# Asking for the next weights nine products ahead instead of six, out of the same twelve buffers

## The chip, the cores and the metric

One core of a Trainium2 chip runs the whole program in one launch. The metric is device time in microseconds (us), smaller is better. Executions of the same program agree within a few tenths of a per cent.

## What is computed

Three stages in a row, all in float32 (the arrays of the last stage's weights come in as 64-bit floats and are turned into 32-bit ones on the core). Cut to what matters:

```python
# attention: 4 x 8 heads, 576 tokens, head size 64, chunks of 64 tokens
scores = scale * q_c @ k_c.T ; attn = softmax(scores) ; x = attn @ v_c      # -> x: 2304 x 512
# mixture of 4 experts, hidden width 1024 each
for e in range(4):
    h = maximum(x @ w1[e], 0)
    out += p[:, e:e+1] * (h @ w2[e])
# gated layer, width 1536
g = x @ w_gate
y = (silu(g) * (x @ w_val)) @ w_out
```

## The kernel before

**Passes, sets and products.** Tokens go through in passes of 768 (`TT` = 384, two halves). There are three passes of the expert stage and then three of the gated stage. A product `x @ W` on a block of 512 input and 256 output columns is done by a Strassen-Winograd scheme: seven products of half size instead of eight (`PRODUCTS`). One such block of weights in one pass is a *set*, and its seven products carry the places i = 0 to 6. Each operand is a sum of blocks of weights, kept as a high and a low part, so a product is six matmuls of 384 columns at L627, L628 and L629 (`half_k`), read from one *weight tile* of 256 KB. These tiles come from the pool `w` of twelve buffers (L789). `product` (L631) uses a tile and lets go of its buffer.

**Where the weight tiles come from.** In the first pass they are split on the core (`make_w`, L406) and stored to memory. In all later passes `load_w` (L413) loads them back with one DMA on the queue of SyncE, SP (issue at L415). The program is written out by hand: Python goes through the list `prods`, one *step* per product, and at each step it records the product, then work put off to this step by `later`, then `prepare` for the product `LEAD` = 6 steps on, and then some tasks. Each engine, and SP's queue of DMAs, does its own instructions strictly in the recorded order.

**A second user of the same twelve buffers.** During the second and third pass, tasks turn the 64-bit weights of the gated stage into split tiles (`make_ops`, L455). Each task loads a raw block on SP (L464) into a place that an earlier task must have left, converts it, and then makes seven tiles with `w_split` (L401), at most one tile a step. A made tile is also taken from the pool `w`. ScalarE (ACT) writes its high part at L125, GpSimd (POOL) its low part at L126, and three steps later SP stores it (L476):

```python
for a, to in stores:
    yield SPLIT
    t = w_split(r, a, f"made_{name}")
    later(3, lambda to=to, t=t: nc.sync.dma_start(to, t.bitcast(F32)))
```

There are 18 such groups of seven, 126 made tiles. A buffer can be written again once its product has run, or once its store has landed.

**What ACT owes TensorE (PE).** After products 0, 2 and 3 of a set ACT copies the sum out of PSUM (`keep`, L609, shown at L611: the tiles p, u and p again). Products 2, 4 and 5 then add into the same bank and have to wait for that copy. Between them stand other products and a gap of 18 matmuls of the second layer (y, L676 to L680; ox and oz at L743 in the gated stage).

**The change of pass.** Seven operands of the next pass's tokens are fetched raw (`x_fetch`, L205, issue at L208) into three buffers (pool `xt`, L1100) and split by ACT and VectorE (DVE) or POOL (`x_split`, L210). The first three are fetched ahead. Operand i + 3 is fetched two steps after product i of the last set, and operand i is split one step after that product, which frees a raw buffer.

**Other transfers on SP.** Second-layer weights of the experts (L515, L531) and of the gated stage (`fetch_wo`, L498, issue at L507), which wait for buffers that PE frees.

Of the kernel before, what the change touches and what calls it, by code (L numbers as in the profile page):

```python
# [91 lines left out]
def attention_moe_gated(  # L92
# [46 lines left out]
    def pass_of(n):  # L139
        part, s, _, _ = sets[n]  # L140
        return s + (NPASS if part == "two" else 0)

    def group_of(n):
        part, s, r, _ = sets[n]
        return (s * NPAIRS + r) // 2 if part == "one" else NPASS * NG1 + (s * NPAIRS2 + r) // 2
# [7 lines left out]
    def part_of(G):  # L153

        if G < NPASS * NG1:
            return (1, *divmod(G, NG1))
        return (2, *divmod(G - NPASS * NG1, NG2))

    now = [0]
    deferred = {}  # L160

    def later(d, f):
        deferred.setdefault(now[0] + d, []).append(f)
# [12 lines left out]
    def x_source(p, b):  # L176
        if b[0] == "b":
            return xs[p][int(b[2]) - 1, :, 2 * int(b[1]) - 2 : 2 * int(b[1])]
        return xt_d[p][int(b[1]) - 1]
# [25 lines left out]
    def x_fetch(p, i):  # L205
        b = PRODUCTS[i][2]
        t = x_raw[p, b] = xt_p.tile([P, 2, TT], F32, tag="xt", name=f"xraw_{b}_{p}")
        nc.sync.dma_start(t, x_source(p, b))  # L208
# [178 lines left out]
    def fetch_w1(n):  # L387
        r = raw1[n] = raw1_p.tile([P, 8, 2 * P], F32, tag="raw1", name=f"raw1_{n}")
        nc.sync.dma_start(r[:, 0:4], w1[weights_of(n)])

    def w_sums(r, engine=None, half=None):
        ops = (
            (S1, A21, A22, ALU.add),
            (S2, S1, A11, ALU.subtract),
            (S3, A11, A21, ALU.subtract),
            (S4, A12, S2, ALU.subtract),
        )
        for o, a, b, op in ops if half is None else ops[2 * half : 2 * half + 2]:
            (engine or nc.vector).tensor_tensor(out=r[:, o], in0=r[:, a], in1=r[:, b], op=op)  # L399
# [6 lines left out]
    def make_w(n, i):  # L406
        a = PRODUCTS[i][1]
        t = wop[n, i] = w_split(raw1[n], a, n)
        later(3, lambda: nc.sync.dma_start(w_d[weights_of(n)][i], t.bitcast(F32)))
        if i == NPROD - 1:  # L410
            del raw1[n]

    def load_w(n, i):  # L413
        t = wop[n, i] = w_p.tile([P, 2, 2 * P], F32R, tag="w", name=f"w_{n}_{i}")
        nc.sync.dma_start(t.bitcast(F32), w_d[weights_of(n)][i])  # L415
# [95 lines left out]
    def fetch_w2(G, j):  # L511
        part, s, g = part_of(G)
        if part == 1 and s > 0:
            t = w2op[G, j] = w2_tile(G, j)
            nc.sync.dma_start(t.bitcast(F32), w2_d[4 * g + j])  # L515
            return
        r = raw2[G, j] = raw2_p.tile([P, DM], F32, tag="raw2", name=f"raw2_{G}_{j}")
        nc.sync.dma_start(r, w2[4 * g + j])
# [148 lines left out]
    def layer2(G):  # L667

        for b in range(BLOCKS):
            pool, tag = y_places[b % len(y_places)]  # L670
            y = pool.tile([P, DM], F32, tag=tag, name=f"y_{G}_{b}")
            c = slice(b % HALF * P, (b % HALF + 1) * P)
            for j in range(4):
                hh, hl = hid[G, j, b // HALF]
                w = w2op[G, j]
                nc.tensor.matmul(y, hh[:, c], w[:, 0], start=(j == 0), stop=False)  # L676
                yield
                nc.tensor.matmul(y, hh[:, c], w[:, 1], start=False, stop=False)  # L678
                yield
                nc.tensor.matmul(y, hl[:, c], w[:, 0], start=False, stop=(j == 3))  # L680
                if j < 3:
                    yield
            gather(G, b, y)
            yield
# [99 lines left out]
    with tc.manual_schedule():  # L784
# [202 lines left out]
        def is_raw(n):  # L987
            return n < NPAIRS + 3
# [27 lines left out]
            later(1 + j, lambda j=j: first_split("t4", j))  # L1016
        later(2, lambda: split_w2(1, 1))

        FIRST, LEAD = 3, 6
        order = []  # L1020
        for n in range(FIRST, len(sets) + 1):
            for these in ((4, 5), (0, 1)), ((6,), (2, 3)):
# [4 lines left out]
        prods = [o for o in order if o is not None]  # L1027

        def last_of_pass(n):
            return 0 <= n < len(sets) - 1 and pass_of(n + 1) != pass_of(n)  # L1030

        def prepare(n, i):
            if is_raw(n):
                if i in (1, 3):
                    w_sums(raw1[n], half=i // 2)
                make_w(n, i)
                if i == NPROD - 1 and is_raw(n + 2):
                    fetch_w1(n + 2)
            else:
                load_w(n, i)  # L1040

        gap = 0
        for o in order:
            if o is None:

                gap += 1
                m = FIRST + (gap - 2) // 2
                G = group_of(m) - 1 if m >= FIRST else 0
                if G == 0:
                    for _ in range(12):  # L1050
                        next(two)
                elif part_of(G)[0] == 2:
                    if gap % 2 == 0 and group_of(m - 1) == G:
                        two = layer_out(G)
                    for _ in range(18):
                        next(two, None)
                else:
                    size = sum(group_of(k) == G + 1 for k in range(len(sets)))
                    if gap % 2 == 0 and group_of(m - 1) == G:
                        two = layer2(G)  # L1060
                    for _ in range(12 * BLOCKS // (2 * size)):
                        next(two)
                continue
            n, i = o
            p = pass_of(n)
            if o == (N1, 0):
                assert not tasks and not running, (len(tasks), len(running))
                raw64_cm.close()
                sg_p = ctx.enter_context(tc.tile_pool(name="sg", bufs=6, side="right"))
                wow_p = ctx.enter_context(tc.tile_pool(name="wow", bufs=2, side="right"))  # L1070
            product(n, i)
            if i == 0 and (n == FIRST or group_of(n) != group_of(n - 1)) and group_of(n) < NPASS * NG1:

                W = NPROD * sum(group_of(k) == group_of(n) for k in range(len(sets)))
                for j in range(2 if n == FIRST else 0, 4):
                    last = W + 2 if group_of(n) < NG1 - 1 else 5 + j * W // 4
                    begin, end = 1 + j * W // 4, 5 + j * W // 4 if j < 3 else last
                    if n == FIRST:
                        begin, end = 2 * j - 3, 4 * j - 3
                    later(begin, lambda G=group_of(n), j=j: fetch_w2(G, j))  # L1080
                    later(end, lambda G=group_of(n), j=j: split_w2(G, j))
            if last_of_pass(n + 1) and i == 5:
                for k in range(3):
                    x_fetch(p + 1, k)
            if last_of_pass(n):

                later(1, lambda p=p, i=i: x_split(p + 1, i))
                if i + 3 < NPROD:
                    later(2, lambda p=p, i=i: x_fetch(p + 1, i + 3))
            for f in deferred.pop(now[0], []):  # L1090
                f()
            if now[0] + LEAD < len(prods):
                prepare(*prods[now[0] + LEAD])
            if rest and now[0] % NPROD < 5:
                stage, a = rest.pop(0)
                stage(a, (psA, "a"))
                if not rest:
                    at_cm.close()
                    y_places.append((psA, "a"))
                    xt_p = ctx.enter_context(tc.tile_pool(name="xt", bufs=3, side="right"))  # L1100
                    w2x_p = ctx.enter_context(tc.tile_pool(name="w2x", bufs=1, side="right"))
                    raw64_cm = ExitStack()
                    raw64_p = raw64_cm.enter_context(tc.tile_pool(name="raw64", bufs=2, side="right"))
                    tasks.append(x_sums(1))
            if o == (NPAIRS + 2, 1):
                tasks += [x_sums(2)] + make64
            elif o == (2 * NPAIRS + 3, 1):
                tasks.insert(0, (y for p in (3, 4) for y in x_sums(p)))
            elif o == (N1 + 5, 4):
                tasks.append(x_sums(5))  # L1110
            elif o == (N1 + 3, 2):
                fetch_wo(NPASS * NG1, 0)
                fetch_wo(NPASS * NG1, 1)
            if not (last_of_pass(n) or last_of_pass(n + 1) and i >= 5 or now[0] - turned[0] < 2):
                run_tasks(2)
            now[0] += 1
# [69 lines left out]
```

## Time and profile before

| | |
|---|---|
| median of 3 runs | 1241.95 us (1239.88 to 1243.53) |
| the profiled execution's own time | 1239.78 us |
| its span in the trace | 1238.0 us |
| PE busy | 1223.6 us, 99% |
| DVE, ACT, POOL busy | 794.0, 538.4, 576.6 us |
| DMA queue of SP | 81.9% of 16 engines' span, 357 MB |
| TensorE clock granted | full speed in all 40 slices |

The span runs from the program's first instruction to its last. A matmul's recorded duration overlaps the next one's, so the engine's idle time and what ended it say more than its busy share. The second and third pass of the experts lie between about 355 and 840 us, the gated stage behind that.

### The profile page before, as it was taken

To read this page: it belongs to the slowest core of one execution; us is meant where nothing else is said; L and a number is where in the kernel's file an instruction comes from. 1 tells how busy PE (TensorE), PEld (TensorE's weight loads), DVE (VectorE), ACT (ScalarE), POOL (GpSimd) and SP (SyncE) were. 2 spreads that over 40 slices of the span, in tenths; PEclk is the share of its full clock that TensorE was granted. 3 is DMA by queue.
4 is the path that set the end of the run, shared out by engine and by line. 5 is a ranking of instruction groups with operands and counts; after the bars stand their busy time and mean duration, and the time that the engine had idled before them with its cause. 6 is when DMAs were issued, how large, how long until landed. Compare 5 with 4: busy or idle time off the path is not lost.

```text
span 1238.0 us, 21120 instructions
## 1 busy us (share of the span) xinstructions
PE 1223.6 (99%) x7216; PEld 1130.2 (91%) x7216; DVE 794.0 (64%) x1360; ACT 538.4 (43%) x1192; POOL 576.6 (47%) x603
## 2 busy tenths in 40 slices
PE   8999999999999999999999999999999999999998
PEld 6888888899888999898889889999999999999998
DVE  6776666666646766765566656455667756685576
ACT  4453434445424454544354344334435344444331
POOL 5554434477517776847376867301432222222221
PEclk9999999999999999999999999999999999999999
DMA  7587786799797999897899999866898797698874
GB/s 239 169 285 269 267 280 226 242 320 354 266 354 270 366 323 351 308 390 268 290 367 331 344 396 310 301 214 229 297 321 297 269 322 262 245 327 293 275 235 154
DMA packets 179562, 359.94 MB, mean 291 GB/s; under 512 B 19184, under 2 KB 46320, under 8 KB 179456
## 3 DMA queue, kind: packets, MB, share of 16 engines
q1 hardware_dynamic: 178528, 357.12, 81.9%
q10 hardware_dynamic: 896, 1.44, 0.4%
q8 instruction: 58, 0.95, 0.3%
q14 instruction: 48, 0.39, 0.1%
q0 software_dynamic: 32, 0.04, 0.0%
HBM read 258.90 MB, written 99.61 MB: 290 GB/s over the span
## 4 chain that ended last, share of the span: by engine, by line
PE 87%; DMA 4%; DVE 3%; issue 2%; ACT 2%; POOL 2%; SPq 1%; POOLq 0%; DVEq 0%; ACTq 0%
PE y L676 10%; PE y L680 10%; PE y L678 9%; PE lx L627 8%; PE lx L629 8%; PE lx L628 8%; PE ox L743 5%; PE oz L743 4%; PE lz L627 4%; PE lz L629 4%; PE lz L628 4%; PE lw L627 2%; PE lw L629 2%; PE lw L628 2%; DMA w<-w 1%
## 5 line engine op out<-in xcount | busy, mean ns | idle before, releaser
L676 PE MATMUL y<-w,hh 128*128 128x512 f32 x576 | 228.2, 396 | 0.0
L680 PE MATMUL y<-w,hl 128*128 128x512 f32 x576 | 226.5, 393 | 0.0
L678 PE MATMUL y<-w,hh 128*128 128x512 f32 x576 | 225.8, 392 | 0.2 <-POOL w L126 0.2
L126 POOL TENSOR_TENSOR ol<-sg,oh 128x384 fp32r<-128x384 f32 x72 | 80.0, 1121 | 307.1 <-ACT oh L125 260.0
L126 POOL TENSOR_TENSOR w<-raw,w 128x256 fp32r<-128x256 f32 (+1 forms) x156 | 143.5, 936 | 149.1 <-ACT w L125 131.7
L562 ACT ACTIVATE hh<-sum_p 128x384 fp32r<-128x384 f32 x90 | 47.2, 525 | 221.9 <-DVE sum_p L615 221.9
L766 DVE SCALAR_TENSOR_TENSOR acc<-y,prob,acc 128x512 f32<-128x512 f32 x126 | 91.2, 744 | 65.7 <-PE y L680 65.6
L680 PEld LDWEIGHTS y<-w,hl 128*128 128x128 f32 x576 | 108.1, 188 | 24.0
L676 PEld LDWEIGHTS y<-w,hh 128*128 128x128 f32 x576 | 108.3, 188 | 21.4 <-issue 1.4
L678 PEld LDWEIGHTS y<-w,hh 128*128 128x128 f32 x576 | 108.3, 188 | 21.2 <-POOL w L126 0.6
L615 DVE TENSOR_TENSOR sum_p<-lx,p 128x384 f32<-128x384 f32 x81 | 45.0, 555 | 93.0 <-PE lx L629 93.0
L563 DVE SCALAR_TENSOR_TENSOR hl<-sum_p,hh 128x384 fp32r<-128x384 f32 x90 | 61.7, 685 | 61.8 <-ACT hh L562 61.8
L126 POOL TENSOR_TENSOR w_made<-raw,w_made 128x256 fp32r<-128x256 f32 x84 | 68.1, 818 | 65.5 <-ACT w_made L125 53.0
L125 ACT ACTIVATE w<-raw 128x256 fp32r<-128x256 f32 (+1 forms) x156 | 67.6, 454 | 5.4 <-DVE raw L399 2.3
L125 ACT ACTIVATE oh<-sg 128x384 fp32r<-128x384 f32 x72 | 36.5, 525 | 70.4 <-DVE sg L576 70.1
L611 ACT COPY u<-lx 128x384 f32<-128x384 f32 x81 | 38.6, 476 | 64.5 <-PE lx L629 64.3
L627 PE MATMUL lz<-b22h,w 128*128 128x384 f32 x162 | 55.9, 345 | 0.9 <-ACT p L611 0.8
L627 PE MATMUL lz<-t1h,w 128*128 128x384 f32 x162 | 55.4, 342 | 1.2 <-DMA w<-w 1.1
L627 PE MATMUL lw<-b21h,w 128*128 128x384 f32 x162 | 54.8, 338 | 0.8 <-DMA w<-w 0.7
L627 PE MATMUL lx<-t2h,w 128*128 128x384 f32 x162 | 55.0, 340 | 0.0
L629 PE MATMUL lx<-t3h,w 128*128 128x384 f32 x162 | 54.9, 339 | 0.0
L615 DVE TENSOR_TENSOR sum_p<-lw,p 128x384 f32<-128x384 f32 x81 | 44.8, 553 | 15.8 <-PE lw L629 12.7
(273 smaller groups left out, 3384.6 us busy)
## 6 DMA issues: line engine op xcount, KB each, us to landing
w<-w SPq DMA_DIRECT2D x567, 256.0 KB, 5.4
w<-w SPq DMA_DIRECT2D x96, 512.0 KB, 6.1
w<-w_made SPq DMA_DIRECT2D x84, 256.0 KB, 5.8
wo_t<-wo_t SPq DMA_DIRECT2D x36, 512.0 KB, 5.1
wo_b<-wo_b SPq DMA_DIRECT2D x27, 512.0 KB, 4.1
raw<-w SPq DMA_DIRECT2D x19, 512.0 KB, 4.1
raw<-w SPq DMA_DIRECT2D x32, 256.0 KB, 4.4
sums<-x SPq DMA_DIRECT2D x40, 192.0 KB, 5.8
```

What stands on the lines that cost most here:

```text
L125: nc.scalar.activation(h, src, AF.Copy)
L126: (lo or nc.vector).tensor_tensor(out=l, in0=src, in1=h.bitcast(F32), op=ALU.subtract)
L563: nc.vector.scalar_tensor_tensor(out=l, in0=src, scalar=0.0, in1=h.bitcast(F32), op0=ALU.max, op1=ALU.subtract)
L615: nc.vector.tensor_tensor(out=t, in0=ps, in1=snap.pop(name), op=ALU.add)
L627: nc.tensor.matmul(ps, w[:, 0, c], xh[:, k], start=f, stop=False, skip_group_check=True)
L628: nc.tensor.matmul(ps, w[:, 0, c], xl[:, k], start=False, stop=False, skip_group_check=True)
L629: nc.tensor.matmul(ps, w[:, 1, c], xh[:, k], start=False, stop=e, skip_group_check=True)
L676: nc.tensor.matmul(y, hh[:, c], w[:, 0], start=(j == 0), stop=False)
L678: nc.tensor.matmul(y, hh[:, c], w[:, 1], start=False, stop=False)
L680: nc.tensor.matmul(y, hl[:, c], w[:, 0], start=False, stop=(j == 3))
L743: nc.tensor.matmul(o, left[:, c], w[:, k, right], start=start and t % 2 == 0 and k == 0 and i == 0, stop=k == 1 and i == 2, skip_group_che ...
L766: nc.vector.scalar_tensor_tensor(out=sum_, in0=y, scalar=p, in1=sum_, op0=ALU.mult, op1=ALU.add)
```

## The change

`prepare` for a product whose weights are loaded is called nine steps ahead. Where the weights are made (first pass), it stays at six. Since the list changes over from made to loaded, a counter `ready` says which product is next, and a step can prepare up to two. The pool `w` keeps its twelve buffers. At a change of pass, operand i + 3 is fetched four steps after product i instead of two; the split stays where it was.

```diff
-        FIRST, LEAD = 3, 6
+        FIRST, LEAD, LEAD_LOADS, X_WAIT = 3, 6, 9, 4
...
         gap = 0
+        ready = [LEAD]
...
                 if i + 3 < NPROD:
-                    later(2, lambda p=p, i=i: x_fetch(p + 1, i + 3))
+                    later(X_WAIT, lambda p=p, i=i: x_fetch(p + 1, i + 3))
             for f in deferred.pop(now[0], []):
                 f()
-            if now[0] + LEAD < len(prods):
-                prepare(*prods[now[0] + LEAD])
+            for _ in range(2):
+                if ready[0] < len(prods):
+                    if ready[0] <= now[0] + (LEAD if is_raw(prods[ready[0]][0]) else LEAD_LOADS):
+                        prepare(*prods[ready[0]])
+                        ready[0] += 1
```

The instructions on PE, DVE, ACT and POOL stand in the same order in both programs. Only SP's queue is in another order; on the other engines what changes is which buffer a weight tile gets, and so what its writer waits for.

**First place: SP's queue in the third make group of the gate weights, second pass.** `w_1` is the weight tile of a product with place 1, the number behind the arrow is the tile in memory, `w_made` a made tile, `raw_0` the raw block that starts a new task. Before:

```order
L515 DMA w_14_2_6017<-w_26_131 128x1024
L476 DMA w_97<-w_made_0_4_5960 128x512
L415 DMA w_0_6020<-w_91 128x512
L464 DMA raw_0_6027<-wg 128x1024 x2
L476 DMA w_97<-w_made_0_6_5981 128x512
L415 DMA w_1_6062<-w_91 128x512
L476 DMA w_97<-w_made_0_7_5999 128x512
L415 DMA w_6_6076<-w_90 128x512
```

With the change:

```order
L415 DMA w_1_5985<-w_91 128x512
L476 DMA w_97<-w_made_0_5_5924 128x512
L415 DMA w_6_6003<-w_90 128x512
L515 DMA w_14_2_6023<-w_26_131 128x1024
L476 DMA w_97<-w_made_0_4_5966 128x512
L415 DMA w_2_6026<-w_91 128x512
L464 DMA raw_0_6033<-wg 128x1024 x2
L476 DMA w_97<-w_made_0_6_5987 128x512
L415 DMA w_3_6068<-w_91 128x512
```

The load of `w_1` from tile 91 stood behind the raw block and a store; it now stands three loads earlier, ahead of both. Raw blocks and stores keep their places among themselves.

**Second place: SP's queue at the change from the first to the second pass of the gated stage.** `xraw` is a raw operand of the next pass: t1, t3, b22 and t4 in this order; `w_3_10949` is the weight tile of the product that uses t1. Before:

```order
L208 DMA xraw_t_4_10870<-xt_75 128x768
L415 DMA w_1_10880<-w_93 128x512
L208 DMA xraw_t_4_10890<-xt_75 128x768
L415 DMA w_6_10893<-w_104 128x512
L415 DMA w_2_10909<-w_93 128x512
L507 DMA wo_t_10911<-wo_t_2_152 128x1024
L208 DMA xraw_b_4_10943<-x_69 128x768
L415 DMA w_3_10949<-w_93 128x512
L208 DMA xraw_t_4_10960<-xt_75 128x768
```

With the change:

```order
L415 DMA w_3_10884<-w_93 128x512
L415 DMA w_4_10895<-w_93 128x512
L208 DMA xraw_t_4_10906<-xt_75 128x768
L415 DMA w_5_10913<-w_93 128x512
L507 DMA wo_t_10915<-wo_t_2_152 128x1024
L208 DMA xraw_t_4_10947<-xt_75 128x768
L415 DMA w_0_10953<-w_94 128x512
L415 DMA w_1_10972<-w_94 128x512
L208 DMA xraw_b_4_10983<-x_69 128x768
L415 DMA w_6_10991<-w_93 128x512
L208 DMA xraw_t_4_11003<-xt_75 128x768
```

The weights for t1 moved from behind the fetch of b22 to ahead of the fetch of t1. The fetch of t3 moved behind one transfer of second-layer weights (`wo_t`), and b22 behind two more loads of weights.

## Rows read from the trace of the kernel before

**Rows 1.** The page's head and part 1: busy us, share of the span, instructions.

```profile
span 1238.0 us, 21120 instructions
PE 1223.6 (99%) x7216; PEld 1130.2 (91%) x7216; DVE 794.0 (64%) x1360; ACT 538.4 (43%) x1192; POOL 576.6 (47%) x603
```

**Rows 2.** Waits of PE, 250 to 1200 us: us in total, times, longest us.

```profile
PE lz L627 <- DMA w<-w: 1.1, 1, 1.1
PE lz L627 <- ACT p L611: 0.8, 2, 0.5
PE lw L627 <- DMA w<-w: 0.7, 1, 0.7
```

**Rows 3.** Waits of PE's weight loads (PEld), whole span.

```profile
PEld lw L627 <- DMA w<-w: 1.4, 2, 1.0
```

**Rows 4.** Chain of waits, 500 to 530 us: start us, us, what.

```profile
516.78 0.71 POOL w_made L126
517.51 0.33 SPq L464
...
518.37 0.42 SPq L476
...
518.84 6.01 DMA w<-w
...
524.89 0.44 PE lw L627
```

**Rows 5.** Chain of waits, 700 to 718 us.

```profile
709.02 0.44 SPq L476
...
709.56 6.23 DMA w<-w
...
715.83 0.44 PE lw L627
```

**Rows 6.** Chain of waits, 944 to 962 us.

```profile
947.40 0.97 DVE t2l L126
...
948.39 6.41 DMA xraw_b<-x
...
954.82 0.85 ACT b22h L125
...
959.82 0.37 ACT p L611
...
960.24 0.44 PE lz L627
```

**Rows 7.** SP's queue in order of time, 940 to 962 us: start, us, instruction.

```profile
943.02 0.32 SPq L208 DMA_DIRECT2D xraw_t<-xt  x1
...
946.18 0.32 SPq L208 DMA_DIRECT2D xraw_t<-xt  x1
...
947.55 0.38 SPq L507 DMA_DIRECT2D wo_t<-wo_t  x1
948.39 0.32 SPq L208 DMA_DIRECT2D xraw_b<-x  x1
948.76 0.42 SPq L415 DMA_DIRECT2D w<-w  x1
```

**Rows 8.** Instructions of line L476: stores of made tiles, who waited, landing.

```profile
L476 SPq DMA_DIRECT2D w<-w_made x84: 319/320/1586, 394.4 to 793.8; - x84
...
  POOL w_made L126: 4.7, 2
  ACT w_made L125: 1.2, 2
...
DMA to landing us min/median/max: 2.0/5.8/8.2
```

**Rows 9.** Stretch 390 to 550 us: all engines, then L627 alone (two a product).

```profile
390.00:550.00 160.00, 159.88 (x800) 144.13 (x799) 110.28 (x166) 80.10 (x179) 118.45 (x124) 1.00 0.92 332
390.00:550.00 160.00, 48.58 (x145) 27.06 (x144) 1.00 0.92 332
```

**Rows 10.** PE and ACT in order of time, 508 to 516 us.

```profile
510.93 0.46 ACT L611 COPY p<-lx 128x384 f32<-128x384 f32 x1
511.28 0.42 ACT L125 ACTIVATE w_made<-raw 128x256 fp32r<-128x256 f32 x1
515.20 0.34 PE L627 MATMUL lx<-t2h,w 128*128 128x384 f32 x1
```

**Rows 11.** DMA issues by line: KB each, median us to landing.

```profile
xraw_t<-xt SPq DMA_DIRECT2D x20, 384.0 KB, 4.5
xraw_b<-x SPq DMA_DIRECT2D x15, 384.0 KB, 6.4
```

## Prediction

> **What bounds the kernel now.** I read the busy shares first. PE is busy for 1223.6 of 1238.0 us [rows 1], so only a change that reaches PE counts, and there is little to win. The next view is what PE waits for between 250 and 1200 us, the part in which weights are loaded and both changed numbers act. Its waits are short and few [rows 2]: 1.1 us once and 0.7 us once for a weight tile, 0.8 us in two pieces for ACT's copy p. The loads into the array show two waits for a weight tile at lw, 1.4 us together [rows 3]. I then followed the chain of waits back from each of these places. The two at lw have one cause. At 517.51 SP could issue a raw block (L464) only when POOL had finished a made tile at 517.49; the store and then the weight load stood behind it in the queue, so the load went out at 518.84, took 6.01 us, and PE started late at 524.89 [rows 4]. At 709.56 it was a store that held the queue, and PE started at 715.83 [rows 5]. The weights were late because SP's queue was blocked, not because memory was slow. The wait of 1.1 us lies at 954 us, in a change of pass: the weight load behind the fetch of b22 could go only at 948.76, since that fetch waited for the raw buffer that DVE freed with t2l at 948.37 [rows 6, 7].
>
> **Part 1: earlier loads.** The first place of the order shows that the load which was late at 524.89 now stands ahead of the raw block and both stores. The same holds for the one at 715.83, since every load moved three products forward. Three products are 6.6 us: in the stretch of 390 to 550 us L627 ran 145 times, two a product, so 72.5 products in 160 us, 2.2 us each [rows 9]. Both delays are smaller than that, so I take both away: **minus 1.4 us** [rows 3]. The bounds are nothing, if the freed buffers come too late to load earlier, and 1.4.
>
> The wait at 954 us goes too, because the weights for t1 now stand ahead of the fetch of t1. But what is late next is known. PE then runs up to b22, which needs ACT's copy p, and ACT makes that copy at 959.82, behind b22h, which waited for the raw operand until 954.80 [rows 6]. PE would be there 1.1 us sooner and wait 1.1 us longer. I count **0**; the upper end of the gain is the 1.1.
>
> **Part 2: raw operands two steps later.** In the second place of the order the fetch of t3 now stands behind `wo_t`, which went out at 947.55, where t3 had gone at 946.18 [rows 7]. That is some 1.8 us later with its own issue. b22 stands behind two more weight loads of 0.42 us each [rows 7], so about 0.9 us later, and the chain from b22 to PE at 960.24 has no slack [rows 6]. Against it stands its flight, 6.41 us in this chain, where operands t land in a median of 4.5 us and operands b in 6.4 [rows 6, 11]; fewer loads would be let go behind it at once. I take **0** here, nearest to the fact that the fetch still cannot start before DVE is done at 948.37. There are five changes of pass, so the bounds are minus 0.5 and plus 4.5 us (5 x 0.9).
>
> **Part 3: the made tiles lose their buffers.** This is the part of the change that the diff does not show. With a lead of six, six of twelve buffers hold weights that are waiting to be used, and six are left for made tiles. A made tile keeps its buffer for three steps until its store is issued, and until the store has landed, a median of 5.8 us [rows 8] or 2.6 products of 2.2 us [rows 9]. In a group of seven, one a step, that is 5.6 buffers: it fits. With a lead of nine, three are left, and 9 + 5.6 = 14.6 are wanted. So in 18 groups ACT and POOL, or SP's loads, must wait for a store to land. I counted the waits in the two built programs. Before, no split of a made tile waits for a store recorded in the same step or the step ahead of it; with the change 20 of 126 do, 12 of them in the same step.
>
> What does ACT's waiting cost PE? In one of these groups ACT copies p at 510.93 and starts a made tile at 511.28, and PE needs that bank at 515.20 [rows 10]. The copy was done at 511.39, so there are 3.8 us of cover at such a place. SP can issue the store at best when PE is through the product before, 2.2 us ahead of the split, since in the changed program most loads in front of the store wait for that product's buffer. The wait is then 5.8 - 2.2 = 3.6 us, just under the cover; with the longest landing, 8.2 us [rows 8], it is 6.0 us, 2.2 us over it. In the kernel before, waits for these stores came to 4.7 and 1.2 us and none reached PE [rows 8]. The bounds are therefore 0 and 12 x 2.2 = 26 us. I take two of the twelve at 1 us over the cover, **plus 2.0 us**, much nearer to the lower end, because a median landing stays covered. POOL's own waits I cost at nothing: it is busy for 118 of 160 us there [rows 9] and owes PE nothing in this stretch but the low parts of operands at a change of pass; without that cover its lag would show in the next group's start.
>
> The Trainium skill, in "DMA: Bandwidth & Descriptors", section "Anatomy of one DMA", puts a transfer at about 2.0 us plus its bytes over 436 GB/s, measured on another issuing path. An estimate from that page for 256 KB is 2.6 us, a buffer would then be held for 4.2 steps, every such wait would stay under the cover, and part 3 would cost nothing: the sum would be minus 1.4. The trace disagrees with the page for a queue this full: the median is 5.8 us and only the shortest, 2.0, comes near it [rows 8].
>
> **Sum.** Minus 1.4, plus 0, plus 0, plus 2.0: **plus 0.6 us** on the profiled execution's 1239.78 us, whose span of 1238.0 us leaves 1.8 outside. It is 2.2 us under the median of the runs, 1241.95. So I predict 1242.6 us.
>
> A measurement of this kernel can tell about 0.3%, 3.7 us; the lines are 1238.2 and 1245.7 us.
>
> **Rivals.**
> - *ACT and POOL are starved of buffers* (slower, 22%). The mechanism is part 3, in the groups between 390 and 800 us. It decides once the waits beyond the cover come to 5.1 us (3.7 + 1.4), 0.43 us for each of the twelve. At 0.6 us each it is 7 us, and the time is 1241.95 - 1.4 + 7 = 1247.6 us. For it: 14.6 buffers wanted of twelve, landings of up to 8.2 us. Against it: the cover, and that loads take part of the shortage, which nine ahead can bear.
> - *The raw operands come late* (slower, 6%). At each of five changes the 0.9 us reaches PE: with parts 1 and 3 as above, 1241.95 + 0.6 + 4.5 = 1247.0 us. Against it: the fetch waits for DVE anyway.
> - *All waits for memory go* (faster, 12%). PE's waits in the stretch are 1.4 + 1.1 + 0.8 = 3.3 us [rows 2, 3]. If all go and part 3 is free, the profiled execution comes to 1236.5 us and the median to 1238.6; it needs another 0.4 us from the median run, which has 2.2 us more to lose than the profiled one, to pass the line. About 1237.9 us then.
> - *The lead is not had* (no change, 12%). In the make groups the freed buffers come so late that the loads start no earlier than before: 12 - 5.6 = 6.4 buffers for loads is a lead of six again. Nothing of the 1.4 is won: 1241.95 + 2.0 = 1244.0 us.
>
> **How the numbers follow.** My forecast has 48%, and with the last rival "within 0.3%" has 60%; faster 12%; slower 28%. The range goes from 1238.8, nearly all waits gone, to 1248.0, just over the two slower cases. It leaves out about one in ten on each side.
>
> **What would show it.** Right: no wait of PE's lw for a weight tile between 250 and 840 us; waits of ACT and POOL at w_made for the stores (L476) grown from 5.9 us to tens of us; PE waiting for ACT's copies or for hl some 2 us more; the wait at 954 us moved to b22. Wrong on part 1: lw still waits. Wrong on part 3: PE's waits for ACT's copies p and u in 390 to 800 us come to over 5 us, or made tiles do not wait at all. Wrong on part 2: ACT's waits at b22h grow by more than 1 us at each change.

## The result, and the profile after

The change made the kernel slower: 1260.53 us (median of 4 runs, 1260.15 to 1261.82) against 1242.24 us for the kernel before on the same chip. The ratio is 1.0148, with a 95% interval of 1.0133 to 1.0163. The forecast was 1242.6 us, no change that could be told, and the range on record ended at 1248.0, so the prediction was wrong.

Where the time went is read from three views. The page's head and part 1 of the changed kernel answer to [rows 1]:

```profile
span 1260.0 us, 21223 instructions
PE 1231.7 (98%) x7216; PEld 1134.6 (90%) x7216; DVE 800.8 (64%) x1360; ACT 538.1 (43%) x1192; POOL 579.4 (46%) x603
```

The profiled span grew by 22.0 us (the medians differ by 18.3). An early group of matmuls of the gated stage dates it: the first ox<-wo_t began at 873.0 us before and at 895.3 us after, 22.3 us later. The next two rows show it, of the kernel before and of the changed one, from the instructions of line L743 (least, median and greatest duration in ns, then first and last start):

```profile
L743 PE MATMUL ox<-wo_t,oh x204: 276/279/385, 873.0 to 1225.5; 128*128 128x256 f32 x102
```

```profile
L743 PE MATMUL ox<-wo_t,oh x204: 276/279/387, 895.3 to 1247.4; 128*128 128x256 f32 x102
```

The stage's first sigmoid (sg, L570) was already as late, 840.4 against 818.1 us. So all of the loss lies ahead of the gated stage. What PE waits for between 250 and 1200 us now, to be held against [rows 2] (us in total, times, longest):

```profile
PE lz L627 <- ACT p L611: 9.6, 7, 3.0
PE y L680 <- DVE hl L563: 4.1, 2, 3.4
PE y L678 <- POOL w L126: 1.3, 1, 1.3
PE lx L627 <- ACT p L611: 0.9, 2, 0.5
PE lx L627 <- ACT u L611: 0.6, 1, 0.6
```

No wait for a weight tile is left. In its place stand waits for ACT's copies, and for hl (the low part of a hidden tile), which DVE makes behind ACT's hh (its high part). What held ACT in the stretch of the made tiles, 380 to 830 us, is the next view (waits of ACT; before, all waits of ACT and POOL for these stores came to 5.9 us, [rows 8]):

```profile
ACT w_made L125 <- DMA w<-w_made: 41.9, 15, 7.6
ACT w_made_wo L125 <- DMA w<-w_made: 24.5, 8, 6.2
...
ACT w_made L125 <- DMA wo_b<-w_made_wo: 11.2, 3, 4.9
...
ACT w_made L125 <- DMA wo_t<-w_made_wo: 6.7, 4, 3.2
ACT w_made_wo L125 <- DMA wo_b<-w_made_wo: 4.2, 4, 1.2
```

A made tile that ACT is about to write waits until the last user of its buffer, another made tile, has been stored and has landed. The five rows add up to 88.5 us; with a sixth of the same kind, 1.7 us, they are 36 waits of 90.2 us. PE's longest wait for the copy p, in the chain of waits between 412 and 422 us, shows one from end to end:

```profile
409.35 7.70 DMA w<-w_made
...
417.13 0.42 ACT w_made_wo L125
```

A store went out at 409.35 and was 7.70 us on its way, ACT stood for it from 410.96 until 417.13, and PE, which needed ACT's copy p for b22, stood for 2.99 us until 417.97. Behind such a wait comes a second cost. Three stretches of the changed kernel, right behind the waits at 415, 500 and 549 us (time, then busy us of PE, PEld, DVE, ACT and POOL with counts, then the granted clock, the share of the DMA engines, and GB/s):

```profile
417.80:421.20 3.40, 3.23 (x10) 3.23 (x11) 1.91 (x3) 0.95 (x3) 3.32 (x4) 0.53 0.90 352
...
503.30:506.60 3.30, 3.30 (x13) 3.30 (x12) 0.70 (x2) 2.83 (x6) 1.09 (x2) 0.51 1.03 385
552.60:557.80 5.20, 5.16 (x14) 4.51 (x15) 1.86 (x2) 1.83 (x3) 3.83 (x5) 0.50 0.97 327
```

TensorE's granted clock was about 0.5 there, its lower level of 1.2 instead of 2.4 GHz. PE was busy for 11.7 of the 11.9 us and, at half the clock, did about half the work, so by estimate 5 to 6 us more were lost.

### The profile page after: what moved, and what is told of

The parts are those of the page before. It is cut to its first block, busy times and chain, and to the rows that moved or that the text cites. A ratio compares the mean times of both kernels' runs of the same rounds, so it can differ in the third digit from the quotient of the medians.

```text
span 1260.0 us, 21223 instructions
## 1 busy us (share of the span) xinstructions
PE 1231.7 (98%) x7216; PEld 1134.6 (90%) x7216; DVE 800.8 (64%) x1360; ACT 538.1 (43%) x1192; POOL 579.4 (46%) x603
## 4 chain that ended last, share of the span: by engine, by line
PE 73%; DMA 10%; POOL 5%; issue 4%; DVE 4%; ACT 2%; SPq 1%; POOLq 0%; ACTq 0%; DVEq 0%
PE y L680 7%; PE y L676 7%; PE y L678 7%; PE lx L627 7%; PE lx L629 7%; PE lx L628 7%; DMA w<-w_made 5%; PE ox L743 5%; PE oz L743 4%; PE lz L627 4%; PE lz L629 3%; PE lz L628 3%; DMA wo_b<-w_made_wo 2%; PE lw L627 2%; PE lw L629 2%
## 5 line engine op out<-in xcount | busy, mean ns | idle before, releaser
L678 PE MATMUL y<-w,hh 128*128 128x512 f32 x576 | 226.1, 393 | 1.3 <-POOL w L126 1.3
L678 PEld LDWEIGHTS y<-w,hh 128*128 128x128 f32 x576 | 108.5, 188 | 22.5 <-POOL w L126 1.8
L676 PEld LDWEIGHTS y<-w,hh 128*128 128x128 f32 x576 | 108.5, 188 | 21.8 <-issue 1.4
L563 DVE SCALAR_TENSOR_TENSOR hl<-sum_p,hh 128x384 fp32r<-128x384 f32 x90 | 69.0, 766 | 88.6 <-ACT hh L562 88.6
L627 PE MATMUL lz<-b22h,w 128*128 128x384 f32 x162 | 57.0, 352 | 9.7 <-ACT p L611 9.6
L125 ACT ACTIVATE w_made<-raw 128x256 fp32r<-128x256 f32 x84 | 34.6, 412 | 74.3 <-DMA w<-w_made 41.9
L627 PE MATMUL lx<-t2h,w 128*128 128x384 f32 x162 | 55.3, 341 | 0.9 <-ACT p L611 0.9
L627 PE MATMUL lx<-t3h,w 128*128 128x384 f32 x162 | 55.3, 341 | 0.6 <-ACT u L611 0.6
L629 PE MATMUL lx<-t3h,w 128*128 128x384 f32 x162 | 55.2, 341 | 0.0
```

The lines of the kernel that those rows point to most:

```text
L125: nc.scalar.activation(h, src, AF.Copy)
L563: nc.vector.scalar_tensor_tensor(out=l, in0=src, scalar=0.0, in1=h.bitcast(F32), op0=ALU.max, op1=ALU.subtract)
L627: nc.tensor.matmul(ps, w[:, 0, c], xh[:, k], start=f, stop=False, skip_group_check=True)
L629: nc.tensor.matmul(ps, w[:, 1, c], xh[:, k], start=False, stop=e, skip_group_check=True)
```

## The experiments

Theory A: nine loads leave three of the twelve buffers for made tiles, ACT waits for stores to land, and PE waits for ACT. Theory B: the later raw operands stall the changes of pass. Theory C: the order of SP's queue makes the stores late, whatever the buffers. All ratios are to the kernel before, on the same chip.

**The raw operands alone.**

```diff
-        FIRST, LEAD, LEAD_LOADS, X_WAIT = 3, 6, 9, 4
+        FIRST, LEAD, LEAD_LOADS, X_WAIT = 3, 6, 6, 4
```

> The changed kernel with the lead of loaded weights put back to six; raw operands of a new pass still fetched four steps later. Theory A (the loss comes from three buffers instead of six being left for the made tiles): as the kernel before, within 0.3% (1238.5 to 1246 us), ACT's waits at made tiles for stores back to about 1 us. Theory B (the later raw operands stall ACT and PE at the changes of pass): slower by most of the 18 us, 1255 us or more. The step of the prediction on raw operands, bounds minus 0.5 to plus 4.5 us, is tested by the same number.

Measured: 1245.12 us, ratio 1.0016 (1.0006 to 1.0027). Theory B does not explain the loss, but the part has a price of about 2 us, where the prediction counted nothing. Its place is the first change of pass, near 300 us, as POOL's instructions in order of time show (start, us, instruction, in brackets the idle time before it and its cause). Of the kernel before:

```profile
303.35 2.04 POOL L126 TENSOR_TENSOR t1l<-xraw_t,t1h 128x768 fp32r<-128x768 f32 x1
```

Of this kernel:

```profile
308.23 1.86 POOL L126 TENSOR_TENSOR t1l<-xraw_t,t1h 128x768 fp32r<-128x768 f32 x1 [2.09 <-ACT t1h L125]
```

In the expert stage the low parts of most raw operands are POOL's work, and at this change POOL also still splits weights for the next pass. t1 is fetched later, POOL stands for 2.09 us, and the splits behind it are late for PE: its wait for POOL's w at y L678 was 0.2 us before and 1.4 us here. Of the 4.9 us between the two starts, 3.0 were there before any fetch was later: the split of b21, two operands earlier, began at 294.27 us in the kernel before and at 297.31 here. So some 1.8 us belong to this change of pass.

**The lead alone.**

```diff
-        FIRST, LEAD, LEAD_LOADS, X_WAIT = 3, 6, 9, 4
+        FIRST, LEAD, LEAD_LOADS, X_WAIT = 3, 6, 9, 2
```

> The changed kernel with the raw operands fetched two steps after the product, as before; the lead of nine stays. Theory A: as the changed kernel, 1256 to 1264 us, PE's waits for ACT's copies at b22 between 400 and 750 us about 8 us as in it. Theory B: back to the time of the kernel before. If both parts lose, it lies between, near 1250 us.

Measured: 1261.05 us, ratio 1.0151 (1.0124 to 1.0177), the whole loss. PE waits 10.0 us for ACT's copy p at lz, ACT up to 8.7 us for one store. The lead carries it.

**The same lead with more room.** Three of every six made tiles go to three other buffers of the same size.

```diff
+            made_count[0] += 1
+            if made_count[0] % 6 < 3:
+                pool, how = (made_p[0], dict(tag="made")) if made_count[0] % 6 == 0 else (raw2_p, dict(tag="raw2"))
...
+                    made_p.append(raw64_cm.enter_context(tc.tile_pool(name="made", bufs=1, side="right")))
```

> The changed kernel, lead nine and raw operands four steps later, but three of every six made tiles come from three other buffers (two of the pool of raw second-layer weights, idle by then, and one new one). Theory A: 9 + 2.8 = 11.8 tiles then share the twelve, no split waits long for a landing, and the time returns to that of the kernel before or 1 to 3 us under it (1238 to 1243 us); PE's waits at lw for weights stay away. Theory C (the stores are late because in SP's queue loads that wait for PE now stand in front of them, whatever buffers there are): still over 1252 us.

Measured: 1241.20 us, ratio 0.9989 (0.9980 to 0.9998). Neither the lead nor the raw operands were touched, and the loss is gone. Waits of ACT for the stores of made tiles are no longer among its waits in this stretch. All five queues have the same order as in the changed kernel, so this is the run that decides for theory A and against C.

**The shortage without the lead.** In the kernel before:

```diff
-            later(3, lambda to=to, t=t: nc.sync.dma_start(to, t.bitcast(F32)))
+            later(6, lambda to=to, t=t: nc.sync.dma_start(to, t.bitcast(F32)))
```

> The kernel before, lead six, with one number changed: a made tile is stored six steps after it is made instead of three, so it keeps its buffer three steps longer, 8.6 instead of 5.6 buffers on an estimate from the same rows, and 6 + 8.6 = 14.6 are wanted of twelve, as in the changed kernel. No load and no raw operand moves ahead. Theory A: slower by 8 to 20 us, with ACT waiting at made tiles for the landing of stores for tens of us. Theories B and C: within 0.5% of the kernel before.

Measured: 1254.27 us, ratio 1.0093 (1.0076 to 1.0110), inside the expected loss. ACT waits for the stores for some 51 us (18.8, 16.3, 13.8 and 1.8). But the way to PE is partly another one. Its waits between 250 and 1200 us:

```profile
PE lz L627 <- DMA w<-w: 3.9, 2, 2.1
PE lx L627 <- DMA w<-w: 3.6, 4, 2.0
PE lz L627 <- ACT p L611: 3.3, 4, 1.5
PE lw L627 <- DMA w<-w: 1.6, 2, 1.3
```

With a lead of six most of the shortage reaches PE through weights: 9.1 us in these rows, 6.3 of them in the stretch of the made tiles, 390 to 830 us, against 3.2 us there for ACT's p and for hl. In the changed kernel that stretch had no wait for weights at all. So the shortage cost time with either lead, but not by the same way.

**One less.**

```diff
-        FIRST, LEAD, LEAD_LOADS, X_WAIT = 3, 6, 9, 4
+        FIRST, LEAD, LEAD_LOADS, X_WAIT = 3, 6, 8, 4
```

> The changed kernel with a lead of eight instead of nine; raw operands four steps later. By the count of buffers 8 + 5.6 = 13.6 are wanted of twelve, 1.6 short instead of 2.6. If the loss grows from the point where twelve are exceeded, 1247 to 1254 us; if it comes only when stores chain to each other through the loads between them (a split then waits for two landings), it is smaller than in proportion, 1243 to 1247 us. A loss that does not come from the buffers would stay near 1258 us.

Measured: 1244.54 us, ratio 1.0020 (1.0004 to 1.0035). With 1.6 buffers too few nearly all of the loss is gone (one of the ten runs took 1253.14). ACT still waits, but 3.8 us at most for the stores w<-w_made against 7.6 (and 5.6 us once for wo_b), and that stays mostly under the cover of [rows 10]. The loss is not in proportion to the shortage.

**Stores two steps sooner.** In the changed kernel:

```diff
-            later(3, lambda to=to, t=t: nc.sync.dma_start(to, t.bitcast(F32)))
+            later(1, lambda to=to, t=t: nc.sync.dma_start(to, t.bitcast(F32)))
```

> The changed kernel with one number changed: a made tile is stored one step after it is made instead of three. Its buffer is free two steps sooner (an estimate of 3.6 buffers instead of 5.6, so 12.6 wanted of twelve), and fewer loads that wait for buffers stand in the queue between the tile and its store. Theory A: most of the loss goes, 1242 to 1248 us, ACT's waits at made tiles for stores under 25 us. Against it: SP must now wait longer for POOL at each store (L476), which holds up the loads behind it; if that decides, over 1252 us with PE waiting for weights.

Measured: 1260.11 us, ratio 1.0135 (1.0119 to 1.0151). A miss for the count of steps. The stores stand sooner in the program, but not on the chip. What SP waits for between 250 and 830 us in this kernel:

```profile
SPq L476 <- POOL w_made L126: 92.0, 51, 10.9
SPq L476 <- POOL w_made_wo L126: 36.5, 24, 6.3
```

SP stands 128.5 us for POOL to finish the tiles, against 23.6 us in the changed kernel (18.4 and 5.2). A store can't go before POOL is done, so ACT still waits 72 us in all, where under 25 were expected, and for one store 10.7 us. PE does not wait for weights, which nine ahead survive. Of the two outcomes written down, the time is that of the second, but PE's waits are ACT's copies as in theory A.

**Stores from POOL's queue.** In the changed kernel:

```diff
-            later(3, lambda to=to, t=t: nc.sync.dma_start(to, t.bitcast(F32)))
+            later(3, lambda to=to, t=t: nc.gpsimd.dma_start(to, t.bitcast(F32)))
```

> The changed kernel, lead nine and the same twelve buffers, but made tiles are stored from POOL's queue instead of SP's, at the same step. A store then no longer stands behind a load that waits for another store's landing. If the loss is the shortage of buffers made long by such chains on SP's queue (theory A with chains): ACT's waits at made tiles for stores fall to less than half of some 90 us, and the time to 1243 to 1252 us. If the shortage alone makes it (each split waits for one landing of 5 to 6 us, wherever it is issued): ACT's waits stay over 60 us and the time over 1254 us. POOL pays for issuing 126 transfers, which no trace so far shows; if that comes to more than its idle time in this stretch, the time is over 1260 us and the run tells nothing.

Measured: 1358.21 us, ratio 1.0935 (1.0920 to 1.0949). By what was written down this run tells nothing on chains in SP's queue, and that question stays open. What it does show, in the instructions of line L476, is where its own time went:

```profile
L476 POOL DMA_DIRECT2D w<-w_made x84: 539/562/765, 400.4 to 915.9; - x84
...
  ACT w_made L125: 125.1, 29
  ACT w_made_wo L125: 81.2, 19
...
DMA to landing us min/median/max: 2.3/4.0/8.7
```

A store costs POOL 0.56 us to issue, 71 us for 126, and the flight got shorter, a median of 4.0 us. Yet ACT's waits for the stores grew to 206 us. So the landing is not what is long here. That the stores are late because POOL, which does its work in order, comes to them late is my reading; no run tests it.

**The version with room, raw operands as before.** The edit of the version with room, and:

```diff
-        FIRST, LEAD, LEAD_LOADS, X_WAIT = 3, 6, 9, 4
+        FIRST, LEAD, LEAD_LOADS, X_WAIT = 3, 6, 9, 2
```

> Lead nine, three other buffers for half of the made tiles, and the raw operands fetched two steps after the product as in the kernel before. With only the later raw operands changed the time rose by 0.16%, about 2 us; if that is the cost of the later fetch, this one is 1 to 3 us under the version with later raw operands, 1238 to 1241 us. If the two only work together (weights ahead of the blocked fetch), it is the same or slower, 1241 to 1244 us.

Measured: 1239.62 us (1238.06 to 1244.10, 12 runs), ratio 0.9982 (0.9971 to 0.9993). This beats both kernels, by about 2 us under the kernel before. PE's waits between 250 and 1200 us (its line numbers are 7 higher):

```profile
PE lz L634 <- ACT p L618: 1.5, 2, 0.8
PE y L685 <- POOL w L126: 0.3, 1, 0.3
PE ox L750 <- DVE acc L723: 0.3, 1, 0.3
```

No wait for weights, none for made tiles, and POOL's w is back at 0.3 us.

**The room without the lead.** The kernel before with the three other buffers.

> The kernel before, lead six, raw operands two steps later, with the three other buffers for half of the made tiles. It tells whether the small gain of lead nine with more room comes from the lead or from the room. If from the lead: as the kernel before within 0.15%, with PE's two waits at lw for weights still there. If from the room: 1 to 3 us faster than the kernel before.

Measured: 1242.02 us, ratio 0.9999 (0.9990 to 1.0007), with PE's wait at lw for weights still there (1.4 us). So the small gain of the last version comes from the lead once it has the room.

**Nine only where no tiles are made.** The same twelve buffers, raw operands as before.

```diff
-                    if ready[0] <= now[0] + (LEAD if is_raw(prods[ready[0]][0]) else LEAD_LOADS):
+                    if ready[0] <= now[0] + (LEAD if prods[ready[0]][0] < N1 else LEAD_LOADS):
```

> The same twelve buffers; lead six for both expert passes whose weights are loaded, nine only for the gated stage, where no tiles are made; raw operands fetched two steps later as before. Theory A: none of the loss, within 0.15% of the kernel before (1240.5 to 1244 us), the wait for weights at the change of pass near 954 us gone or moved to ACT's copy. Were the lead itself harmful, in any stage, over 1246 us.

Measured: 1242.12 us, ratio 1.0009 (0.9999 to 1.0019). PE's wait for weights at the change of pass is gone there, and 0.8 us for ACT's copy p at b22 stand in its place. The loss belongs to the stage with made tiles; in the gated stage the longer lead neither costs nor brings anything that can be measured.

**Eight, raw operands as before.**

```diff
-        FIRST, LEAD, LEAD_LOADS, X_WAIT = 3, 6, 9, 4
+        FIRST, LEAD, LEAD_LOADS, X_WAIT = 3, 6, 8, 2
```

> The same twelve buffers, lead eight, raw operands fetched two steps later as before. With raw operands four steps later a lead of eight came to 1244.5 us, as much as that part alone (1245.1). If that part was all of its loss, this one is at the kernel before or up to 3 us under it, 1239.5 to 1243 us, with no PE wait at lw for weights. If lead eight has a loss of its own, 1244 to 1247 us.

Measured: 1244.82 us, ratio 1.0023 (1.0010 to 1.0035). A miss: I had put lead eight's 2 us down to the raw operands. Lead eight has a small loss of its own. PE waits 1.6 us for hl and 3.0 us for ACT's copies, and no longer for weights.

## Why the prediction was wrong, point by point

- **What bounds the kernel, part 1: right.** The two waits at lw [rows 3 to 5] are gone, and every wait of PE for a weight tile in the stretch with them. The 1.4 us were read from the loads into the array [rows 3]; PE's own idle time at lw was 0.7 us [rows 2], so that is nearer to what there was to win in this stretch. The version with room and raw operands as before has no wait of PE for weights between 250 and 1200 us and is about 2 us faster than the kernel before.
- **The wait at 954 us: right.** It moved to b22, as said. In the changed kernel t2l again ends just ahead of the fetch of b22 and the chain between 966 and 984 us has the same links as [rows 6]:

```profile
970.67 5.96 DMA xraw_b<-x
976.65 0.86 ACT b22h L125
...
981.65 0.38 ACT p L611
982.07 0.44 PE lz L627
```

  PE goes on at 982.07, 21.8 us after its 960.24 of before, while ox had begun 22.3 us late: 0.5 us won at most.
- **Part 2, counted at 0: mis-sized.** It cost about 2 us by itself, within the bounds of minus 0.5 to plus 4.5. Beside a lead of eight or nine out of the twelve buffers the price does not show (1244.54 with it against 1244.82 without, 1260.53 against 1261.05); with room it does (1241.20 against 1239.62). The price was looked for at the changes of pass of the gated stage. It fell due at the first change, in the expert stage, where POOL splits the operands and weights at once. The step said that a fetch could not start before its buffer was free anyway; that holds for b22, not for t1, for whose fetch ACT stood 2.72 us in the run with the raw operands alone.
- **Part 3, plus 2.0: this is the step that failed.** The mechanism was named right, 14.6 buffers wanted of twelve, and it was the first rival, with 22%. What failed is the price: two waits of PE, 1 us each. PE had nine between 390 and 830 us, 13.2 us together, where the kernel before had 0.7, and the clock fell behind three of them. Three links of the price broke.

  First, the wait of ACT. It was put at twelve places and at 3.6 us, a store's flight of 5.8 less a head start of 2.2, since SP was taken to issue the store as soon as PE was through the product before. There were 36 waits. On average they were shorter than that, 2.5 us, but seven were 4.1 to 7.6 us long. The median flight hardly moved (5.8 us before, 5.6 after); in the long waits the store went out late, or flew long, or both. Ahead of PE's 2.99 us the head start was 1.6 us and the flight 7.70. Ahead of ACT's longest wait, 7.6 us until 817.96, SP had stood 3.5 us at a load of weights, and the store went out 2.4 us after ACT had come for it; ahead of the next longest, 6.7 us until 688.93, SP had stood 3.3 us at a raw block for POOL. Neither of these two reached PE: it has no wait in the 10 us behind them. What did grow is SP's standing at loads of weights for the landing of stores of made tiles, 44.5 us between 380 and 830 us, where it had been 6.1 us in all before. Waits of SP, of the kernel before (whole span) and of the changed one:

```profile
SPq L415 <- DMA w<-w_made: 6.1, 17, 1.5
```

```profile
SPq L415 <- DMA w<-w_made: 44.5, 31, 7.1
```

  The next store stood behind each of these loads. The prediction had only the other half of it, that loads would take part of the shortage and could bear it: PE never waited for one. SP's waits at raw blocks for POOL's w_made did not grow (34.9 us before, 23.7 after, 380 to 830 us). How much of ACT's waits comes from that queue and how much from POOL's lateness was not settled; the run meant for it told nothing.

  Second, the cover. The 3.8 us were read at one copy of p, after product 0 [rows 10]. Other places had less already in the kernel before. At b22, where five of PE's nine waits fell, ACT's copy once ended 1.0 us before PE needed the bank (ACT and PE of the kernel before, in order of time):

```profile
680.20 0.46 ACT L611 COPY p<-lz 128x384 f32<-128x384 f32 x1
681.66 0.33 PE L627 MATMUL lz<-b22h,w 128*128 128x384 f32 x1
```

  The cover was also spent once for each wait, while ACT's waits follow each other in a group of seven: it stood 4.08 us until 496.67 and 3.21 us until 501.35, and the copy p behind the second left PE standing for 1.79 us until 502.19.

  Third, the sum knew one way to PE, the copies. A third of the 13.2 us, 4.1, was for hl. Its longest wait, 3.4 us, in the chain of the changed kernel between 535 and 556 us:

```profile
545.14 0.42 ACT w_made_wo L125
...
547.31 0.42 ACT hh L562
...
547.75 0.56 DVE hl L563
548.31 0.92 DVE neg L445
...
549.25 1.10 DVE top L446
...
550.72 1.40 DVE acc L766 x2
552.12 0.47 DVE hl L563
...
552.64 0.80 PE y L680
```

  ACT came off its last wait at 545.14 and made hh late; DVE, which does its own work in order, then had parts of the conversion of the 64-bit weights (neg, top) and two sums (acc) ahead of the hl that PE needed.
- **The clock was not in the sum.** Before, the granted clock was at full speed in all slices of the page. Here it fell to half three times behind PE's waits, which cost 5 to 6 us; the prediction had no term for it.
- **The sum of what was measured.** PE's waits between 390 and 830 us grew from 0.7 to 13.2 us (8.1 for p at lz, 4.1 for hl, 0.6 and 0.4 for copies at lx). With 5 to 6 us of clock and 1.7 us at the first change of pass (PE's matmul behind POOL's late w began at 313.05 before and 314.79 after) that is 19 to 20 of the 22 us of the profiled span. The rest is not attributed.
- **What decided the chances.** Part 3 put its price near the lower end, and with it the slow rival at 22%, also because in the kernel before no wait for these stores reached PE [rows 8]. By the prediction's own count that row was taken with 11.6 of twelve buffers in use. It says that the edge had not been passed; it says nothing on the price behind it.

## What to carry to other kernels

Count the users of a pool before a prefetch is made longer: the buffers that a longer lead holds are taken from whoever shares the pool, and what was slack for the loads becomes a wait on an engine that is needed elsewhere. When a queue works in order, look for loads that may wait for a store and stand ahead of the next store of its kind; here SP stood 44.5 us at such loads, though no run shows what these alone cost. If a row shows no wait at nearly full occupancy, price the far side of the edge by the longest flight, several in a row, the least cover instead of one, and a clock that drops.

## What the runs showed of the hardware

In the changed kernel the granted clock fell to half three times, right behind PE's three longest waits (3.0 and 1.8 us for p, 3.4 us for hl), and stayed there for 3.3 to 5.2 us, though PE was busy again at once. Not every such wait was followed by it: with the stores two steps sooner PE stood 3.4 us until 428.58 and the granted clock stayed at 1.00, and with the lead alone it stood 2.1 us until 481.75 and 1.8 us until 502.10 with the same outcome. A store from POOL's queue took POOL 0.56 us to issue, where SP took 0.32 us at least and 0.39 in the median in the changed kernel. A store of 256 KB landed after 5.6 us in the median from SP's queue, and after 4.0 us from POOL's in a kernel that was 8% slower than the changed one.
